# A fused attention and mixture kernel: the experts' second product in blocks of pairs of groups, for two of three token blocks

## The chip, the cores and the metric

The program runs on one core of a Trainium2 chip. The time is the device time of one execution, in microseconds (us); lower is better. The engines are TensorE (PE in the rows; its weight loads are PEld), VectorE (DVE), ScalarE (ACT), GpSimd (POOL) and SyncE (SP), which here issues all transfers.

## The reference, cut to what matters

```
# attention over 4 x 8 heads, 576 positions, block causal; then
x = attn.transpose(0, 2, 1, 3).reshape(2304, 512)
h = x @ w_in; x = (h * cos(h)) @ w_out             # first mixture layer
P = exp(x @ w_gate - max), 8 rounds of row and column normalisation
for e in range(8):                                 # second layer: all experts, all tokens
    h = maximum(x @ w1[e], 0)                      # 2304 x 512 @ 512 x 1024
    ye = h @ w2[e]                                 # 2304 x 1024 @ 1024 x 512
    out += P[:, e:e+1] * ye
```

## The kernel before, in words

Attention and the first layer take the first 600 us or so. The rest is the experts' loop, which the change touches. All products are in float32 precision by split operands: a tensor is held as a high part (rounded, `AF.Copy` to fp32r on ScalarE) and a low part (the difference, a subtraction on VectorE or GpSimd), and each product is three matmuls, high x high, high x low, low x high (`mm3`, L522 to L524).

The tokens are cut into three blocks of 768 (`HB`; `TB` is half of one), the 1024 hidden units of an expert into four slices `j` of 2 x 128 (`NJ`), so that there are 3 x 8 x 4 = 96 groups `(tb, e, j)`. Groups 0 to 31 are the first token block, 32 to 63 the second, 64 to 95 the third; all three use the same weights. A group does:

- The first product, x @ w1, as seven block products by the scheme of Strassen and Winograd: `A11 B11`, `S1 T1`, `S2 T2`, `A12 B21`, `S3 T3`, `A22 T4`, `S4 B22`, called P1 to P7 here in that order. The A and S are blocks and sums of blocks of w1, the B and T of the tokens. Each is 6 matmuls of 384 columns into the PSUM tiles `hx`, `hy`, `hz`. `hx` is accumulated over P1, P3, P5 and P6 and `hy` over P2 and P7; ScalarE copies `hx` out (`c`) behind P1, P3 and P5, so P3, P5 and P6 each wait for a copy, and VectorE adds `hy` to the third copy, for which P7 waits.
- ReLU and split of the four hidden quarters (`hidden_block`: `hh` on ScalarE, `hl` on VectorE).
- The second product of the group before, `y(g - 1, t)` for six token tiles t: 12 matmuls of 512 columns into `acc`, then VectorE adds P times `acc` to `oa` (L1006). `ys(0)` and `ys(1)` stand behind P5, `ys(2)` to `ys(5)` behind P7.
- The weights of the next group (`Weights(g + 1)`): the sums S1 to S4 on GpSimd, the splits `wbh`, `wbl`, `wah`, `wal` of w1 and `wv` of w2. `wload(g + 2)` loads two 512 KB tiles `stg` for the group after that. Every token block does this anew. All these tiles come out of one pool of 16 buffers (`wp`, tag `w`).

Ahead of a new token block `tprep` forms T1 to T4 of its tokens in ten sums on GpSimd and four splits, spread over the nine groups before it. The order of instructions on each engine is the order of the code (`manual_schedule`); each engine works through its own list and waits for what an instruction needs. At the end the last `y` calls run alone, and `oa` goes out.

## Time and profile before

| | |
|---|---|
| time, median of 3 runs | 2123.76 us (2123.02 to 2125.22) |
| the profiled execution: time, and its span | 2122.82 us, 2121.0 us |
| busy share of the span: TensorE, VectorE, ScalarE, GpSimd | 100%, 69%, 46%, 41% |
| mean transfer rate over the span | 72 GB/s |
| granted TensorE clock | 1.00 |

The span is the time from the first instruction to the last. Shares are averages over stages: attention, the first layer and the 96 groups have different loads.

### The profile page before, as it was taken

What the parts mean: (1) busy time and instruction counts of PE and PEld (TensorE: products, weight loads), DVE (VectorE), ACT (ScalarE), POOL (GpSimd) and SP (SyncE); (2) the same over time, 40 slices, a digit from 0 to 9 for tenths busy, and PEclk for the clock granted to TensorE, in tenths of its full rate; (3) what the DMA queues carried; (4) which work ended last, traced back from release to release, by engine and by line L of the source; (5) the groups of instructions that cost most, each with busy time, mean ns of one, the idle gap of its engine ahead of it and who ended that gap; (6) DMA issues with size and microseconds to landing.
All of it is one profiled execution on the core that took longest, in us unless ns stands there. A gap on an engine that the chain in (4) does not pass through costs nothing.

```text
span 2121.0 us, 29776 instructions
## 1 busy us (share of the span) xinstructions
PE 2112.4 (100%) x10959; PEld 1888.5 (89%) x10959; DVE 1456.0 (69%) x2411; ACT 981.8 (46%) x1852; POOL 875.8 (41%) x793
## 2 busy tenths in 40 slices
PE   9999999999999999999999999999999999999999
PEld 7888999999988888888988988889889888888898
DVE  7887876566768666666766666666776666666665
ACT  7887774344453444344343433433434344433342
POOL 4543233333334443435644434334554343343441
PEclk9999999999999999999999999999999999999999
DMA  6774320000011121211213212212113121121120
GB/s 168 186 190 127 101 89 1 6 11 30 11 50 60 66 74 60 78 62 60 80 46 108 76 60 74 66 60 80 60 62 107 60 74 67 60 80 60 62 78 30
DMA packets 77185, 152.84 MB, mean 72 GB/s; under 512 B 33232, under 2 KB 36816, under 8 KB 77040
## 3 DMA queue, kind: packets, MB, share of 16 engines
q1 hardware_dynamic: 77040, 150.95, 22.8%
q8 instruction: 86, 1.41, 0.3%
q14 instruction: 59, 0.48, 0.1%
HBM read 136.91 MB, written 4.87 MB: 67 GB/s over the span
## 4 chain that ended last, share of the span: by engine, by line
PE 92%; issue 4%; POOL 2%; DVE 1%; ACT 0%; DMA 0%; POOLq 0%; DVEq 0%
PE acc L522 13%; PE acc L524 13%; PE acc L523 13%; PE acc L774 7%; PE hx L524 6%; PE hx L522 6%; PE hx L523 6%; PE o L358 4%; PE hy L522 3%; PE hy L524 3%; PE hy L523 3%; PE h L522 2%; PE h L524 2%; PE h L523 2%; POOL jl L728 2%
## 5 line engine op out<-in xcount | busy, mean ns | idle before, releaser
L633 POOL TENSOR_TENSOR wv<-stg,wv 128x512 fp32r<-128x512 f32 x190 | 327.6, 1745 | 798.6 <-ACT wv L632 789.4
L522 PE MATMUL acc<-wv,hh 128*128 128x512 f32 x1152 | 456.7, 396 | 0.2 <-DVE oa L1000 0.2
L524 PE MATMUL acc<-wv,hl 128*128 128x512 f32 x1152 | 455.6, 395 | 0.0
L523 PE MATMUL acc<-wv,hh 128*128 128x512 f32 x1152 | 454.4, 394 | 0.0
L1006 DVE SCALAR_TENSOR_TENSOR oa<-acc,P,oa 128x512 f32<-128x512 f32 x540 | 378.6, 739 | 5.9 <-PE acc L524 4.3
L977 ACT ACTIVATE hh<-c 128x384 fp32r<-128x384 f32 x288 | 151.2, 525 | 411.2 <-DVE c L1065 167.6
L978 DVE SCALAR_TENSOR_TENSOR hl<-c,hh 128x384 fp32r<-128x384 f32 x288 | 164.9, 573 | 175.9 <-ACT hh L977 175.9
L524 PEld LDWEIGHTS acc<-wv,hl 128*128 128x128 f32 x1152 | 216.0, 187 | 53.8
L523 PEld LDWEIGHTS acc<-wv,hh 128*128 128x128 f32 x1152 | 215.9, 187 | 43.8
L522 PEld LDWEIGHTS acc<-wv,hh 128*128 128x128 f32 x1152 | 216.1, 188 | 43.1 <-DVE oa L1000 0.3
L1058 DVE TENSOR_TENSOR c<-hz,c 128x384 f32<-128x384 f32 x96 | 53.4, 556 | 195.8 <-PE hz L524 195.8
L1045 ACT ACTIVATE c<-hx 128x384 f32<-128x384 f32 x95 | 46.9, 494 | 267.5 <-PE hx L524 267.5
L728 POOL TENSOR_TENSOR jl<-raw,jh 128x512 fp32r<-128x512 f32 x63 | 92.3, 1466 | 189.5 <-ACT jh L723 169.5
L624 DVE TENSOR_TENSOR wal<-s,wah 128x1024 fp32r<-128x1024 f32 x89 | 159.7, 1794 | 0.0
L522 PE MATMUL hx<-th,wah 128*128 128x384 f32 x384 | 128.6, 335 | 0.0
L524 PE MATMUL hx<-th,wal 128*128 128x384 f32 x384 | 128.5, 335 | 0.0
L524 PE MATMUL hy<-xh,wal 128*128 128x384 f32 x384 | 128.5, 335 | 0.0
L522 PE MATMUL hy<-xh,wah 128*128 128x384 f32 x384 | 128.4, 334 | 0.0
L523 PE MATMUL hx<-tl,wah 128*128 128x384 f32 x384 | 128.3, 334 | 0.0
L523 PE MATMUL hy<-xl,wah 128*128 128x384 f32 x384 | 128.3, 334 | 0.0
L978 DVE SCALAR_TENSOR_TENSOR hl<-hx,hh 128x384 fp32r<-128x384 f32 x96 | 53.4, 557 | 104.4 <-ACT hh L977 101.7
L522 PE MATMUL h<-xh,jh 128*128 128x384 f32 x368 | 123.6, 336 | 0.0
(248 smaller groups left out, 4877.6 us busy)
## 6 DMA issues: line engine op xcount, KB each, us to landing
stg<-in_w_b_dram SPq DMA_DIRECT2D x192, 512.0 KB
st<-in_qk_dram SPq DMA_DIRECT2D x64, 144.0 KB
cw<-in_w_a_dram SPq DMA_DIRECT2D x17, 512.0 KB
v<-in_v_dram SPq DMA_DIRECT2D x31, 160.0 KB
tt<-inv SPq DMA_DIRECT2D x32, 144.0 KB
out_dram<-oa SPq DMA_DIRECT2D x18, 256.0 KB
kb<-qb SPq DMA_DIRECT2D x31, 144.0 KB
qb<-qa SPq DMA_DIRECT2D x31, 144.0 KB
```

The source lines that it names most:

```text
L358: nc.tensor.matmul(o[:, q0:q1], vt[:, c], e, start=c == 0, stop=True, skip_group_check=c > 0)
L522: nc.tensor.matmul(ps, lh, rh, start=first, stop=False, skip_group_check=go_on)
L523: nc.tensor.matmul(ps, lh, rl, start=False, stop=False, skip_group_check=go_on)
L524: nc.tensor.matmul(ps, ll, rh, start=False, stop=last, skip_group_check=go_on)
L624: eng.tensor_tensor(out=self.al, in0=self.s, in1=self.ah.bitcast(F32), op=ALU.subtract)
L633: eng.tensor_tensor(out=t[:, DM:2 * DM], in0=src, in1=t[:, 0:DM].bitcast(F32), op=ALU.subtract)
L728: eng.tensor_tensor(out=lo, in0=raw[units[n][1]][:, part * DM:(part + 1) * DM], in1=hi.bitcast(F32), op=ALU.subtract)
L774: nc.tensor.matmul(acc[half, b][:, at:at + w_], w[:, s], h[:, t0:t0 + w_], start=f == 0 and i == 0 and at == 0, stop=f == F1 - 1 and i == ...
L977: nc.scalar.activation(hh, src, AF.Relu)
L978: nc.vector.scalar_tensor_tensor(out=hl, in0=src, scalar=0.0, in1=hh.bitcast(F32), op0=ALU.max, op1=ALU.subtract)
L1006: nc.vector.scalar_tensor_tensor(out=o, in0=acc, scalar=p, in1=o, op0=ALU.mult, op1=ALU.add)
L1058: nc.vector.tensor_tensor(out=c[0], in0=z, in1=c[0], op=ALU.add)
```

## The change: what it does

The first token block stays as it was, but what it makes of the weights is kept. `store` writes the four split tiles of w1 of each group to DRAM (`W1D`, 1.84 MB a group), and `differences` replaces, on VectorE and in place, the w2 half of `stg` by four differences of its blocks and writes them to DRAM (`TD`, 0.52 MB a group). `hidden_block(g, 3)` and `hidden_block(g, 1)` move behind `ys(2)` and `ys(3)`; the pairs `hh`, `hl` now lie in shared tiles `hs`.

The second and third blocks load the split w1 from `W1D`, so the sums and splits of w1 fall away. The second product is done for pairs of groups p = (2p, 2p + 1): with the two groups the contraction is 2 x 256 deep, and the product is seven block products `X1`, `Y1`, `X2`, `Z`, `X3`, `Y2`, `X4` of 256 x 256 blocks, each for three token tiles. The 21 pieces (`TURN`), called items here, have 6 matmuls of 256 columns each; 11 of them stand between P1 to P7 of the next even group, 10 between those of the next odd group (`pair_group`). Their operands are, on the left, the hidden blocks A11, A12, A22 and their sums S1 to S4 (`both` on VectorE, then `high` on ScalarE and `low` on VectorE, 128 x 768 each), and on the right seven blocks of w2 (`w2_split`: high on ScalarE, low on GpSimd), loaded from DRAM into three or four places. Results are added to `oa` by 21 VectorE instructions of 256 columns (`collect`). Behind the last group follow two rounds of `pair_group` with items alone; at group 32 the old `y` calls stand between the products, and at group 33 nothing does.

```diff
+        W1D = [drw.tile([128, 14 * HK], F32, name=f"w1d{g}") for g in range(NA)]
+        TD = [drw.tile([128, 4, 2, HK], F32, name=f"td{p}") for p in range(NA // 2)]
...
+            def store(self):
+                for (at, n), t in zip(PARTS, (self.bh, self.bl, self.ah, self.al)):
+                    nc.sync.dma_start(out=W1D[self.g][:, at:at + n], in_=t[:, 0:n].bitcast(F32))
+            def differences(self, part, eng=nc.vector):
+                a, b = (t[:, DM:2 * DM] for t in stg[self.g])
+                b11, b12, b21, b22 = a[:, 0:HK], a[:, HK:2 * HK], b[:, 0:HK], b[:, HK:2 * HK]
+                for out, in0, in1 in (((b11, b12, b11), (b12, b12, b22)), ((b22, b22, b11), (b21, b21, b22)))[part]:
+                    eng.tensor_tensor(out=out, in0=in0, in1=in1, op=ALU.subtract)
+                if part:
+                    p, k = divmod(self.g, 2)
+                    for i, t in enumerate((a, b)):
+                        nc.sync.dma_start(out=TD[p][:, 2 * i:2 * i + 2, k, :],
+                                          in_=t.rearrange("p (o n) -> p o n", n=HK))
...
+        def w2_split(p, o):
+            if (p, o) in W2:
+                t, raw = W2[p, o], raws.pop((p, o))
+                nc.scalar.activation(t[:, 0:DM], raw, AF.Copy)
+                nc.gpsimd.tensor_tensor(out=t[:, DM:2 * DM], in0=raw, in1=t[:, 0:DM].bitcast(F32), op=ALU.subtract)
+                w2_load(raw)
...
+        TURN = [("X1", 0), ("X1", 1), ("X1", 2), ("Y1", 0), ("Y1", 1), ("Y1", 2), ("X2", 0), ("X2", 1), ("X2", 2),
+                ("Z", 0), ("Z", 1), ("X3", 0), ("X3", 1), ("X3", 2), ("Y2", 0), ("Y2", 1), ("Z", 2),
+                ("X4", 0), ("X4", 1), ("X4", 2), ("Y2", 2)]
...
+            def multiply(self):
+                name, t = self.todo.pop(0)
+                a, b, row, col = ITEMS[name]
+                ps, w, s = self.place(name, t), W2[self.p, b], slice(t * 128, (t + 1) * 128)
+                for k in range(2):
+                    new = k == 0 and name in ("X1", "Y1", "Z") and t != 1
+                    rh, rl = (w[:, i * DM + k * HK:i * DM + (k + 1) * HK] for i in range(2))
+                    mm3(ps, self.h[a][:, k, s], self.l[a][:, k, s], rh, rl, new, k == 1, go_on=True)
+                if t:
+                    self.collect(name, t, row, col)
+                if t == 1:
+                    self.collect(name, 0, row, col)
...
+        def pair_group(g, old, new, splits, ys):
...
+            if now:
+                product(g, x, "S2", "T2", False)
+                nc.scalar.activation(c[1], x, AF.Copy)
+                splits("T2")
+            if old:
+                if k == 0:
+                    old.high("S2")
+                else:
+                    old.high("A22")
+            if now and k:
+                w2_split(p, "B11")
+            items(1)
+            if old:
+                if k == 0:
+                    old.both("S4", "A12", "S2", ALU.subtract)
+                else:
+                    old.low("A22")
+            if now:
+                z = psz.tile([128, TB], F32, tag="z", name="hz")
+                product(g, z, "A12", "B21", True)
+                nc.vector.tensor_tensor(out=new.get("A11", k), in0=z, in1=c[0], op=ALU.add)
+                if k:
+                    new.relu("A11")
+                    new.high("A11")
+            if old and k == 0:
+                w2_split(p - 1, "T3")
+            if old and k == 0:
+                old.low("S2")
+            items(2)
+            if now:
+                product(g, x, "S3", "T3", False)
+                nc.scalar.activation(c[2], x, AF.Copy)
+                nc.vector.tensor_tensor(out=new.get("A22", k), in0=yy, in1=c[2], op=ALU.add)
...
                 product(g, x, "S3", "T3", False)
                 gate("S3")
+                Weights(g).differences(0)
                 nc.scalar.activation(c[2], x, AF.Copy)
                 nc.vector.tensor_tensor(out=c[2], in0=yy, in1=c[2], op=ALU.add)
-                hidden_block(g, 3, c[2])
                 splits("T3")
             ys(0)
             gate("y0")
+            Weights(g).differences(1)
...
             ys(2)
+            if now:
+                hidden_block(g, 3, c[2])
             if w and g:
                 w.lo_a(nc.gpsimd if g < 6 or left == 1 else nc.vector)
             ys(3)
+            if now:
+                hidden_block(g, 1, c[1])
...
             if w and g:
                 w.v(1)
+                w.store()
```

In the rows that follow, `p_...` is an item's PSUM tile, `w_...` a loaded or split weight tile, `raw` a hidden block, and `xh`, `xl` as the output or the weights of an item are the first token block's columns of these tensors, which are free by then and hold the items' left operands.

On TensorE, in a group of the second or third block before, the second product stands behind P5 in runs of 512 columns:

```order
L522 MATMUL hx<-th,wah 128x384
L523 MATMUL hx<-tl,wah 128x384
L524 MATMUL hx<-th,wal 128x384
L522 MATMUL acc<-wv,hh 128x512
L523 MATMUL acc<-wv,hh 128x512
L524 MATMUL acc<-wv,hl 128x512
```

At such a place after the change, an item stands between two products:

```order
L522 MATMUL hx<-th,w_16310 128x384
L523 MATMUL hx<-tl,w_16310 128x384
L524 MATMUL hx<-th,w_16479 128x384
L522 MATMUL p_16696<-w_16484,xh 128x256
L523 MATMUL p_16696<-w_16484,xh 128x256
L524 MATMUL p_16696<-w_16484,xl 128x256
L522 MATMUL hy<-xh,w_16480 128x384
L523 MATMUL hy<-xl,w_16480 128x384
L524 MATMUL hy<-xh,w_16481 128x384
```

The 72 matmuls of 512 columns of two groups have become 126 of 256, in runs of 6 or 12 between runs of 6 of 384; each still has a weight load of its own.

On VectorE, in a group of the first block, from the read of `hz` (P4) on; before:

```order
L1058 TENSOR_TENSOR c<-hz,c 128x384
L978 SCALAR_TENSOR_TENSOR hl<-c,hh 128x384
L613 TENSOR_TENSOR wbl<-stg,wbh 128x512
L615 TENSOR_TENSOR wbl<-stg,wbh 128x256
L1065 TENSOR_TENSOR c<-hy,c 128x384
L978 SCALAR_TENSOR_TENSOR hl<-c,hh 128x384
L1006 SCALAR_TENSOR_TENSOR oa<-acc,P,oa 128x512 x2
```

and with the change, with SyncE's list of such a group below it (before, SyncE had only the two loads of `stg` a group there):

```order
L1351 TENSOR_TENSOR c<-hz,c 128x384
L1001 SCALAR_TENSOR_TENSOR hs<-c,hs 128x384
L617 TENSOR_TENSOR wbl<-stg,wbh 128x512
L619 TENSOR_TENSOR wbl<-stg,wbh 128x256
L650 TENSOR_TENSOR stg<-stg 128x256 x2
L1359 TENSOR_TENSOR c<-hy,c 128x384
L1029 SCALAR_TENSOR_TENSOR oa<-acc,P,oa 128x512
```

```order
L654 DMA td_2418<-stg 128x2x256 x2
L590 DMA stg<-in_w_b_dram 128x1024 x2
L643 DMA w1d_2394<-wbh 128x768
L643 DMA w1d_2394<-wbl 128x768
L643 DMA w1d_2394<-wah 128x1024
L643 DMA w1d_2394<-wal 128x1024
```

Two differences stand ahead of the read of `hy` that P7 waits for, two more behind the first `oa`, and the loads of `stg` stand behind the stores of the differences in SyncE's list.

On VectorE with the change, in an even group of the second or third block (nothing like it stands there before), from `low` of S1 to the items X2:

```order
L1113 TENSOR_TENSOR xh<-raw,xl 128x768
L1162 SCALAR_TENSOR_TENSOR oa<-p_19027,P,oa 128x256 x2
L1162 SCALAR_TENSOR_TENSOR oa<-p_19053,P,oa 128x256
L1125 TENSOR_TENSOR raw<-raw 128x768 x2
L1223 TENSOR_TENSOR raw<-hz,c 128x384
L1113 TENSOR_TENSOR xl<-raw,xl 128x768
L1162 SCALAR_TENSOR_TENSOR oa<-p_19071,P,oa 128x256 x2
L1162 SCALAR_TENSOR_TENSOR oa<-p_19101,P,oa 128x256
```

S2 and S4 (L1125) stand behind the three collects of X1, and `low` of S2 (the second L1113), which X2 needs, behind the read of `hz`.

## Rows read from the trace of the kernel before

**Rows 1.** The page: span, busy time, granted clock and transfers in 40 slices.

```profile
span 2121.0 us, 29776 instructions
PE 2112.4 (100%) x10959; PEld 1888.5 (89%) x10959; DVE 1456.0 (69%) x2411; ACT 981.8 (46%) x1852; POOL 875.8 (41%) x793
...
PEclk9999999999999999999999999999999999999999
...
GB/s 168 186 190 127 101 89 1 6 11 30 11 50 60 66 74 60 78 62 60 80 46 108 76 60 74 66 60 80 60 62 107 60 74 67 60 80 60 62 78 30
```

**Rows 2.** The page: shares of the chain of work that ended last.

```profile
PE 92%; issue 4%; POOL 2%; DVE 1%; ACT 0%; DMA 0%; POOLq 0%; DVEq 0%
```

**Rows 3.** One line's instructions (one a group), 1105 to 2105 us: ns least/median/most, first, last.

```profile
L1058 DVE TENSOR_TENSOR c<-hz,c x64: 540/557/558, 1107.0 to 2097.5; 128x384 f32<-128x384 f32 x64
```

**Rows 4.** Busy time by engine in stretches (an early, a later, a second-block group; a load).

```profile
core 0: us, PE busy (x) PEld busy (x) DVE busy (x) ACT busy (x) POOL busy (x), PEclk, DMA share, GB/s
622.00:637.70 15.70, 15.70 (x82) 14.11 (x81) 11.53 (x26) 9.88 (x20) 8.92 (x8) 1.00 0.19 68
772.50:788.20 15.70, 15.70 (x80) 14.04 (x79) 10.33 (x17) 6.25 (x12) 6.33 (x7) 1.00 0.20 68
1119.29:1135.01 15.72, 15.72 (x80) 14.06 (x79) 10.34 (x17) 6.25 (x12) 6.35 (x7) 1.00 0.40 128
772.50:776.50 4.00, 4.00 (x25) 4.00 (x24) 2.07 (x4) 1.81 (x4) 3.92 (x5) 1.00 0.77 262
```

**Rows 5.** VectorE in order of time, the last `y` calls: start, us, instruction, [idle before].

```profile
2111.74 0.75 DVE L1006 SCALAR_TENSOR_TENSOR oa<-acc,P,oa 128x512 f32<-128x512 f32 x1 [0.65 <-PE acc L524]
...
2117.34 0.75 DVE L1006 SCALAR_TENSOR_TENSOR oa<-acc,P,oa 128x512 f32<-128x512 f32 x1 [0.65 <-PE acc L524]
```

**Rows 6.** The chain in order of time, first layer: 12 matmuls of 512, 12 of 256.

```profile
541.28 4.19 PE acc L774 x24
545.47 0.17 PE h L522
```

**Rows 7.** TensorE in order of time, attention: four matmuls of 256 columns, other weights each.

```profile
151.57 0.28 PE L330 MATMUL sq<-qb,kb 128*128 128x256 f32 x1
...
152.06 0.37 PE L330 MATMUL sr<-qb,kb 128*128 128x448 f32 x1
```

**Rows 8.** Their weight loads in order of time.

```profile
151.69 0.19 PEld L330 LDWEIGHTS sq<-qb,kb 128*128 128x128 f32 x1
151.82 0.19 PEld L331 LDWEIGHTS sq<-qa,ka 101*128 101x128 f32 x1
```

**Rows 9.** Groups of instructions: line, operation xcount | busy us, mean ns | idle before.

```profile
L1006 DVE SCALAR_TENSOR_TENSOR oa<-acc,P,oa 128x512 f32<-128x512 f32 x540 | 378.6, 739 | 5.9 <-PE acc L524 4.3 <-ACT oa L1005 1.5
L1065 DVE TENSOR_TENSOR c<-hy,c 128x384 f32<-128x384 f32 x96 | 52.7, 549 | 0.0
L1045 ACT ACTIVATE c<-hx 128x384 f32<-128x384 f32 x95 | 46.9, 494 | 267.5 <-PE hx L524 267.5
L632 ACT ACTIVATE wv<-stg 128x512 fp32r<-128x512 f32 x192 | 109.5, 616 | 0.0
L645 POOL TENSOR_TENSOR tt<-tt,xl 128x768 f32<-128x768 f32 x6 | 11.1, 1846 | 0.2
```

**Rows 10.** Single lines: ns least/median/most, first and last start (splits of three shapes).

```profile
L70 DVE TENSOR_TENSOR tl<-tt,th x9: 944/957/1556, 519.8 to 1602.4; 128x768 fp32r<-128x768 f32 x9
L624 DVE TENSOR_TENSOR wal<-s,wah x89: 1220/1807/1814, 561.9 to 2091.4; 128x1024 fp32r<-128x1024 f32 x89
L633 POOL TENSOR_TENSOR wv<-stg,wv x190: 1292/1300/2282, 615.3 to 2092.1; 128x512 fp32r<-128x512 f32 x190
L67 ACT ACTIVATE th<-tt x9: 828/831/841, 518.9 to 1601.0; 128x768 fp32r<-128x768 f32 x9
```

**Rows 11.** VectorE in order of time, group from about 772.4 us: behind P4, and its last part.

```profile
779.06 0.42 DVE L615 TENSOR_TENSOR wbl<-stg,wbh 128x256 fp32r<-128x256 f32 x1
779.40 0.55 DVE L1065 TENSOR_TENSOR c<-hy,c 128x384 f32<-128x384 f32 x1
...
786.51 1.81 DVE L624 TENSOR_TENSOR wal<-s,wah 128x1024 fp32r<-128x1024 f32 x1
```

**Rows 12.** ScalarE in order of time, start of the same group.

```profile
774.61 0.41 ACT L609 ACTIVATE wbh<-stg 128x256 fp32r<-128x256 f32 x1
775.73 0.49 ACT L1050 ACTIVATE c<-hx 128x384 f32<-128x384 f32 x1 [0.70 <-PE hx L524]
```

**Rows 13.** All engines in order of time: P4's last matmul, the next, P4's reader.

```profile
1200.84 0.33 PE L524 MATMUL hz<-xh,wbl 128*128 128x384 f32 x1
...
1201.01 0.33 PE L522 MATMUL hx<-th,wah 128*128 128x384 f32 x1
...
1201.28 0.56 DVE L1058 TENSOR_TENSOR c<-hz,c 128x384 f32<-128x384 f32 x1 [2.26 <-PE hz L524]
```

More of the change, by code (lines that the diff above doesn't have):

```diff
@@ L581, in wload @@
         def wload(g):
-            if g < NG:
+            if g < NA:
                 _, e, j = groups[g]
@@ L916, in moe1 @@
                         leftover[n]()
-        moe1()
+            return w0, w1
+        w0, w1 = moe1()
         fin = ctx.enter_context(tc.tile_pool(name="fin", bufs=1))
@@ L1008, in y, with w1_tiles @@
                 nc.sync.dma_start(out=out[row * 128:(row + 1) * 128, :], in_=o)
-        tgen, at = None, ""
-        for g in range(NG + 1):
-            now, w = g < NG, Weights(g + 1) if g + 1 < NG else None
+        W2 = {}
+        B_OPS = {"B11": (0, 0), "B21": (NJ, 0), "B22": (NJ, HK)}
+        T_OPS = {"T1": 0, "T3": 1, "T4": 2, "T2": 3}
+        def w1_tiles(g, some):
+            if g < NG:
+                for i in some:
+                    W2[g, i] = wp.tile([128, 2 * DM], F32R, tag="w", name="w1")
@@ new lines, in w1_load @@
+        def w1_load(g, some):
+            if g < NG:
+                for i in some:
+                    at, n = PARTS[i]
+                    nc.sync.dma_start(out=W2[g, i][:, 0:n].bitcast(F32), in_=W1D[g % NA][:, at:at + n])
+                if max(some) == 3:
+                    bh, bl, ah, al = (W2.pop((g, i)) for i in range(4))
+                    wa[g] = {n: (ah, al, i * HK) for i, n in enumerate(("S1", "S2", "S3", "S4"))}
+                    wa[g] |= {n: (bh, bl, i * HK) for i, n in enumerate(("A11", "A12", "A22"))}
@@ new lines, in w2_tiles, with w2_load @@
+        def w2_tiles(p, ops):
+            if 2 * p < NG:
+                for o in ops:
+                    W2[p, o] = wp.tile([128, 2 * DM], F32R, tag="w", name="w2")
+        W2_ORDER = ("B11", "T1", "T2", "B21", "T3", "B22", "T4")
+        raws, queue = {}, [(p, o) for p in range(NA // 2, NG // 2) for o in W2_ORDER]
+        def w2_load(place):
+            if queue:
+                p, o = queue.pop(0)
+                _, e, j = groups[2 * p]
+                raws[p, o] = place
+                dst = place.rearrange("p (k n) -> p k n", n=HK)
+                if o in B_OPS:
+                    f, c = B_OPS[o]
+                    src = w_b[e, j + f:j + f + 2, :, DM + c:DM + c + HK].rearrange("f p n -> p f n")
+                else:
+                    src = TD[p % (NA // 2)][:, T_OPS[o]]
+                nc.sync.dma_start(out=dst, in_=src)
@@ new lines, in w2_split @@
+        def w2_split(p, o):
[4 more added lines that the diff above has]
+                w2_load(raw)
+        halves = [t[:, c, 0:HB].rearrange("p (k n) -> p k n", n=TB) for t in (xh, xl) for c in range(NC)]
+        ITEMS = {"X1": ("A11", "B11", 0, 0), "Y1": ("S1", "T1", 1, 1), "X2": ("S2", "T2", 0, 1),
+                 "Z": ("A12", "B21", 0, 0), "X3": ("S3", "T3", 1, 1), "Y2": ("S4", "B22", 0, 1),
+                 "X4": ("A22", "T4", 1, 0)}
@@ new lines, in attention_moe_kernel, with last_ys @@
+        tgen, at = None, ""
+        pairs = {}
+        used = {(2 * (NA - 1) + i) % 3 for i in range(2)}
+        places = [f"hs{i}" for i in range(6) if i % 3 not in used]
+        rest = list(range(2 * TT))
+        def last_ys():
+            if rest:
+                y(NA - 1, rest.pop(0))
+                if not rest:
+                    places.extend(f"hs{i}" for i in range(6) if i % 3 in used)
+        for g in range(NG + 2):
+            now, w = g < NA, Weights(g + 1) if g + 1 < NA else None
@@ L1027, in splits @@
                     at = next(tgen, "")
+            if g >= NA:
+                p = g // 2
+                if g == NA:
+                    more = fin.tile([128, 4 * HK], F32, tag="s", name="s")
+                    w2_load(more[:, 0:DM])
+                    w2_load(more[:, DM:2 * DM])
+                    w2_load(post.tile([128, S], F32, tag="lt", name="raw", bufs=1)[:, 0:DM])
+                if 2 * p < NG and p not in pairs:
+                    pairs[p] = Pair(p)
+                pair_group(g, pairs.get(p - 1), pairs.get(p), splits, last_ys)
+                sums(1 + g % 2)
+                continue
             def ys(t):
@@ L1080, in attention_moe_kernel @@
                 nc.vector.tensor_tensor(out=c[1], in0=yy, in1=c[1], op=ALU.add)
-                hidden_block(g, 1, c[1])
                 gate("c1")
                 wload(g + 2)
+                if g >= NA - 2:
+                    w1_tiles(g + 2, range(4))
+                    w1_load(g + 2, range(4))
             ys(2)
+            if now:
+                hidden_block(g, 3, c[2])
             if w and g:
@@ L1087, in attention_moe_kernel @@
             ys(3)
+            if now:
+                hidden_block(g, 1, c[1])
             if w and g:
```

145 lines of the change are left out of this document (140 added, 5 removed).

## The prediction

> **What bounds the kernel now.** I read the page first. TensorE is busy for the whole span, and its granted clock is 1.00 in every slice, the upper level of 2.4 GHz [rows 1]; a busy PE need not be PE at its peak, so I looked at what ends last: TensorE holds 92% of the chain, GpSimd 2%, VectorE 1%, transfers nothing [rows 2]. Then the groups: the instruction that comes once a group starts 64 times between 1107.0 and 2097.5 us, so a group takes 990.5 / 63 = 15.72 us [rows 3], and in a stretch of that length TensorE is busy throughout while VectorE has 10.3 us, ScalarE 6.3 and GpSimd 6.4 [rows 4]. So in the two changed blocks a microsecond taken from TensorE's list is a microsecond gained, as long as nobody else then ends last.
>
> **What TensorE loses and gets.** A token tile of the old second product is 12 matmuls of 512 columns. With nothing else to do at the end, its reader comes every (2117.34 - 2111.74) / 4 = 1.400 us [rows 5], so 0.1167 us per 256 columns, or 0.2333 a matmul. Six tiles are 8.40 us, which leaves 15.72 - 8.40 = 7.32 us for P1 to P7, 1.046 each.
>
> A pair of groups gets 126 matmuls of 256 columns for 72 of 512, that is 32,256 columns for 36,864. What one of them costs decides the change. From below: 24 alternating matmuls take 4.19 us [rows 6], less 12 x 0.2333 leaves 0.116 each. From above: in attention four of 256, each with other weights, take (152.06 - 151.57) / 4 = 0.1225 [rows 7]. A weight load lasts 0.19 us; were loads one behind another, 126 of them would take 23.9 us and the pair would be far slower than before, but they start 0.13 apart, overlapping [rows 8], so they don't set the pace. I take 0.1175: a product's two matmuls with the same weights are nearer to the first case. Then 126 x 0.1175 = 14.8 us, and a pair takes 2 x 7.32 + 14.8 = 29.44 us for 31.44. That is 2.0 us a pair, **64 us in 32 pairs** (0.116: 70 us; 0.1225: 44 us). The change has no other source of gain: the sums and splits of w1 that fall away lie on engines that wait.
>
> The Trainium skill's page "TensorE: Matmul & The Clock Gate", section "Back-to-back issue gap", lists 518 cycles for 512 columns and 262 for 256, 0.216 and 0.109 us at 2.4 GHz. The rows show 0.233 for the first, and they decide; by the page's pair of figures the gain would be 72 x 0.216 - 126 x 0.109 = 1.8 us a pair, 58 us, much the same.
>
> **Whether the other engines keep up with a pair of 29.4 us.** VectorE: 21 collects of 256 columns, 6 sums of 384, 4 sums and 7 low parts of 768. A collect of 512 takes 0.739, a sum of 384 from PSUM 0.549, a low part of 768 undisturbed 0.957 [rows 9, 10]; at about 1.04 ns an element (0.957 less 0.549 over 384 is 1.06) a collect of 256 takes 0.47. Together 9.9 + 3.3 + 10.5 = 23.7 us of 29.4. ScalarE: 8 copies or ReLUs of 0.494, 9 of 768 at 0.83, 7 splits at 0.616, together 15.7. GpSimd: 7 low parts of 1.30, together 9.1. Transfers: 2 x 1.84 + 7 x 0.26 = 5.5 MB, at the 262 GB/s that a load of `stg` reaches [rows 4] 21 us. None is the bound by its sum, so what is left is the order.
>
> I walked the lists of both groups with these durations and 0.27 us from TensorE's going on to a reader's start [rows 13]. Two places are tight. In the odd group, ScalarE has ReLU and high part of A11 (1.66 us) in front of the third copy, for which P6 waits: P4 ends at 6.99 us, VectorE's sum at about 8.3 (the low part of A22 stands before it), the copy at about 10.5 to 10.7, and P6 is due at 10.85. In the even group X2 is due at 9.44 and the low part of S2 comes at about 9.25. Margins of 0.2 us. Behind P6 stand all of TensorE's later items.
>
> What makes them uncertain is GpSimd. The low part of `wal` takes 1.22 us at least and 1.807 in the median, when GpSimd works at `wv`; GpSimd's own goes from 1.300 to 2.282 [rows 10]. So VectorE instructions with both inputs in SBUF and GpSimd's wait for each other. All 11 of the pair's 768-wide VectorE instructions are of that kind. From below such meetings cost nothing; from above one whole GpSimd split, 1.30 us, a pair. The splits stand in GpSimd's list just behind the tight VectorE instructions, so mostly VectorE comes first. I take 0.25 us a pair, **8 us**.
>
> The Trainium skill's page "SBUF — State Buffer", section "Who interferes with whom", says that a VectorE instruction with two SBUF inputs and a GpSimd one that reads SBUF exclude each other for their whole length. The trace agrees (1.22 to 1.807 us). By that rule the price depends only on who comes first, which is my second rival.
>
> **Transition and tail.** At group 33 no old work stands between the products. P6 follows P5 at once, but must wait for the sum of A11, ReLU, high part and copy: 0.27 + 0.55 + 0.83 + 0.83 + 0.49 = 2.97 us and some signals from the end of P4, less P5's 1.05: 2 us. Group 32 has its six old tiles before P5, so P6 waits 0.27 + 0.49 there, 0.8. Together **3 us**. At the end 21 items (14.8 us) run without products between them, and S1's sum, high and low (0.96 + 0.83 + 0.96, behind VectorE's other sum) have only three items of X1, 2.1 us, to hide under; the same for S2. I count 2 us for each, **4 us**; below zero is excluded, since the old tail had no wait but the last reader's.
>
> **The first block.** It does the old work and more. VectorE gets four differences of 256 columns, 0.42 each [rows 11], 1.7 us on 10.3 of 15.7 [rows 4]. Two stand before the sum that P7 waits for: that sum, at 779.40, 7.0 us into the group, moves to about 8.0, less what the moved `hidden_block` spares; it ends at 8.6 and P7 is due at 9.07. So hidden, except where GpSimd or VectorE is late already: the first six groups, with 11.5 us on VectorE and low parts on GpSimd [rows 4], and the nine with `tprep`'s sums of 1.85 us on GpSimd [rows 9]. From 0 to 1.7 us in 5 groups and 0.6 in 9, 0 to 14; I take **4 us**. The same ten sums stand in GpSimd's list in the second block, ahead of the pairs' splits: 0 to 18 us if each shows, I take **4 us**.
>
> Transfers: 1.05 MB in and 2.36 MB out a group, 3.4 MB. The wait that is new: SyncE's loads of `stg` for g + 2 stand behind the stores of the differences, which wait for VectorE, about 10 us into the group. Behind them the four stores wait too, but nobody waits for those soon. At 262 GB/s differences and loads (1.57 MB) take 6 us and land by about 17, that is 1.3 us into the next group, where ScalarE needs the second half at 774.61 - 772.4 = 2.2 [rows 12]; late by more than about 0.9, it holds the copy at 3.3 and P5. So hidden with 1 us to spare.
>
> **The sum.** 2122.8 (the profiled execution: 1.8 us around its span, 0.9 under the median of the runs) - 64 + 3 + 4 + 8 + 4 + 4 = 2081.8; on the median's footing **2083 us**, 1.9% faster. A kernel like this can be told from no change at about 0.2%, 4 us.
>
> **The rivals.**
> - *Slower: the first block is bound by transfers.* The most that the trace moved for longer is 190 GB/s in a slice of 53 us [rows 1]; with a third of it short packets, but stores to DRAM of this size it doesn't show at all. At 190, 3.4 MB take 17.9 us, so the next loads land late, group after group: 32 x 2.2 = 70 us, for 2149. It decides from 3.4 MB in 15.72 + 41 / 32 = 17.0 us, 200 GB/s. Against it: 262 over the 4 us of a load with the engines busy 77%. 8%.
> - *VectorE's chain becomes the bound of the pairs.* If GpSimd comes first once a pair, 32 x 1.3 = 42 us for 8: 2117; twice a pair would be 2158. For it: margins of 0.2. Against it: the order above. 17%, a third of it within 0.2% or slower.
> - *Nothing shows but transition and tail, at 0.116:* 2123.8 - 70 + 7 = 2061. 12%.
> - Something else that ends slower (a wait that I didn't see in the transition's 11 buffer changes): 3%.
>
> My forecast has 60%, between 2066 and 2100. Faster by over 0.2%: 0.60 + 0.11 + 0.12 = 0.83; within: 0.05; slower: 0.12. The range reaches from the third rival to the second: 2062 to 2116.
>
> **What the changed profile would show.** Matmuls of 256 columns start 0.116 to 0.12 apart; a pair takes 29.4 to 30 us, against 31.44. TensorE's idle time lies at P6 of odd groups and at X2, a few tenths each; at group 33 and at the end, 2 to 4 us. Groups 6 to 22 still take 15.72. Wrong would be: groups of the first block over 16 us (transfers or the differences), pairs over 30.5 with TensorE waiting for VectorE's low parts (the lock), or 256-column matmuls 0.13 apart.

## The result and the profile after

The changed kernel takes **2098.43 us** (median of 4 runs, 2097.37 to 2099.77) where the kernel before takes 2123.39 beside it: a ratio of 0.988, 95% interval 0.9867 to 0.9892. The direction and the range hold; the forecast of 2083 is 15.4 us too low. The profiled execution took 2099.2 us with a span of 2097.3.

The page of the changed kernel, its parts on busy time, slices, chain and groups (those that answer to [rows 1, 2, 9]):

```profile
span 2097.3 us, 34781 instructions
PE 2067.8 (99%) x12687; PEld 1944.3 (93%) x12687; DVE 1573.7 (75%) x2733; ACT 1046.8 (50%) x1852; POOL 832.5 (40%) x631
...
GB/s 167 185 186 133 108 91 1 6 11 31 1 106 196 205 226 217 210 228 215 206 218 235 170 197 182 197 180 184 165 178 182 206 203 173 187 201 179 191 174 111
...
PE 92%; DVE 5%; DMA 1%; issue 1%; ACT 1%; POOL 0%; SPq 0%; DVEq 0%; ACTq 0%
...
L1162 DVE SCALAR_TENSOR_TENSOR oa<-p,P,oa 128x256 f32<-128x256 f32 x648 | 280.7, 477 | 66.2 <-PE p L524 64.4
```

TensorE still holds 92% of the chain, but VectorE now has 5% where it had 1% [rows 2], and transfers 1% where they had nothing. Transfers reach 235 GB/s in a slice and lie above the 190 of [rows 1] for ten slices in a row. The collect of 256 columns costs 0.477 us, as forecast (0.47).

The sum of A11, one a group in the two changed blocks (it answers to [rows 3]: ns least/median/most, first and last start), the busy time in the stretch of one undisturbed pair [rows 4], and, in that pair, the first of twelve matmuls of 256 columns and the matmul that follows the twelve, in order of time [rows 6, 7]:

```profile
L1223 DVE TENSOR_TENSOR raw<-hz,c x64: 548/551/559, 1125.3 to 2065.7; 128x384 f32<-128x384 f32 x64
```

```profile
1254.80:1284.40 29.60, 29.60 (x212) 29.60 (x211) 22.43 (x40) 14.55 (x25) 11.00 (x8) 1.00 0.55 188
```

```profile
1263.45 0.28 PE L522 MATMUL p<-w,xh 128*128 128x256 f32 x1
...
1264.88 0.34 PE L522 MATMUL hx<-th,w 128*128 128x384 f32 x1
```

A group takes (2065.7 - 1125.3) / 63 = 14.93 us in the mean, for 15.72. Undisturbed pairs take less: from the first matmul of P2 to that of the next group it is 15.153 us in an even group and 14.433 in an odd one, so a pair is 29.587 us (sums of the unrounded times), with TensorE busy throughout. A matmul of 256 columns is (1264.88 - 1263.45) / 12 = 0.119 us; from the pair it is (29.587 - 2 x 7.32) / 126 = 0.1186.

Where the rest went shows in a ledger of the two traces, by the first matmul of P2 in each group (us):

| stretch | before | after | difference |
|---|---|---|---|
| start to group 0 | 596.66 | 597.48 | +0.8 |
| groups 0 to 5 | 98.19 | 109.35 | +11.2 |
| groups 6 to 31 | 408.72 | 410.81 | +2.1 |
| groups 32 and 33 | 31.44 | 25.84 | -5.6 |
| groups 34 to 55 | 345.84 | 326.03 | -19.8 |
| groups 56 to 64 | 141.48 | 146.45 | +5.0 |
| groups 65 to 94 | 471.75 | 443.80 | -28.0 |
| group 95 to the end | 26.94 | 37.52 | +10.6 |

Two stretches stand out. Groups 0 to 5 lose 11 us, and groups 56 to 64, which at the pace of an undisturbed pair would take 5 x 15.153 + 4 x 14.433 = 133.5 us, take 13.0 more. GpSimd makes the sums of `tprep` for the third block from the end of group 55 on, and the splits follow in group 63, so these are the groups that hold them.

What TensorE waits for, the four largest rows (engine, what, us in total, times, longest):

```profile
PE p L524 <- DVE xl L1113: 7.7, 6, 2.1
PE hx L522 <- ACT c L1343: 5.2, 3, 2.1
PE hy L522 <- DVE c L1359: 2.1, 3, 0.8
PE hx L522 <- ACT c L1234: 2.0, 2, 1.8
```

The first row is low parts that come late, mostly in groups 56 to 62, the second P5 in the first groups, the third P7 in groups 0, 24 and 28, the fourth mostly P6 in group 33. They add up to 17 us; a part of the loss is no wait but the lower clock behind one, as shown below. The four executions of the changed kernel have mean granted clocks of 0.998, 0.997, 0.995 and 0.995, in the order of their times from 2097.37 to 2099.77 us, where the kernel before has 1.00. The waits that I had expected in every pair, at P6 of odd groups and at X2, are not among them.

### The profile page after: what moved, and what is told of

It reads as the page before. It is cut to its first block, busy times and chain, and to the rows that moved or that the text cites. A ratio compares the mean times of both kernels' runs of the same rounds, so it can differ in the third digit from the quotient of the medians.

```text
span 2097.3 us, 34781 instructions
## 1 busy us (share of the span) xinstructions
PE 2067.8 (99%) x12687; PEld 1944.3 (93%) x12687; DVE 1573.7 (75%) x2733; ACT 1046.8 (50%) x1852; POOL 832.5 (40%) x631
## 4 chain that ended last, share of the span: by engine, by line
PE 92%; DVE 5%; DMA 1%; issue 1%; ACT 1%; POOL 0%; SPq 0%; DVEq 0%; ACTq 0%
PE acc L794 10%; PE p L524 7%; PE p L523 7%; PE p L522 7%; PE hx L522 6%; PE hx L523 6%; PE hx L524 6%; PE o L358 4%; PE acc L522 4%; PE acc L524 4%; PE acc L523 4%; PE h L522 3%; PE h L524 3%; PE h L523 3%; PE hy L522 3%; PE hy L523 3%
## 5 line engine op out<-in xcount | busy, mean ns | idle before, releaser
L1078 POOL TENSOR_TENSOR w<-s,w 128x512 fp32r<-128x512 f32 x150 | 237.3, 1582 | 418.7 <-ACT w L1077 399.4
L1162 DVE SCALAR_TENSOR_TENSOR oa<-p,P,oa 128x256 f32<-128x256 f32 x648 | 280.7, 477 | 66.2 <-PE p L524 64.4
L524 PE MATMUL p<-w,xl 128*128 128x256 f32 x894 | 253.9, 284 | 7.7 <-DVE xl L1113 7.7
L523 PE MATMUL p<-w,xh 128*128 128x256 f32 x834 | 235.0, 282 | 0.0
L522 PE MATMUL p<-w,xh 128*128 128x256 f32 x834 | 234.6, 281 | 0.0
L637 POOL TENSOR_TENSOR wv<-stg,wv 128x512 fp32r<-128x512 f32 x62 | 111.8, 1823 | 223.3 <-ACT wv L636 223.3
L524 PEld LDWEIGHTS p<-w,xl 128*128 128x128 f32 x894 | 170.6, 191 | 9.1 <-DVE xl L1113 8.9
L523 PEld LDWEIGHTS p<-w,xh 128*128 128x128 f32 x834 | 158.1, 190 | 0.0
L522 PEld LDWEIGHTS p<-w,xh 128*128 128x128 f32 x834 | 157.7, 189 | 0.0
L522 PE MATMUL acc<-wv,hs 128*128 128x512 f32 x384 | 154.0, 401 | 0.9 <-DVE oa L1023 0.9
L524 PE MATMUL acc<-wv,hs 128*128 128x512 f32 x384 | 152.8, 398 | 0.0
L523 PE MATMUL acc<-wv,hs 128*128 128x512 f32 x384 | 152.5, 397 | 0.0
L522 PE MATMUL p<-w,xl 128*128 128x256 f32 x510 | 145.1, 284 | 1.0 <-ACT xl L1109 1.0
L523 PE MATMUL p<-w,xl 128*128 128x256 f32 x510 | 145.0, 284 | 0.0
L1029 DVE SCALAR_TENSOR_TENSOR oa<-acc,P,oa 128x512 f32<-128x512 f32 x168 | 122.7, 742 | 13.1 <-PE acc L524 12.8
L522 PE MATMUL hx<-th,w 128*128 128x384 f32 x384 | 129.5, 337 | 2.0 <-ACT c L1234 2.0
L524 PE MATMUL hx<-th,w 128*128 128x384 f32 x384 | 128.7, 335 | 0.0
L524 PE MATMUL p<-w,xh 128*128 128x256 f32 x450 | 127.8, 284 | 0.2 <-DVE xh L1113 0.2
```

Of the source, the lines that this page charges most:

```text
L522: nc.tensor.matmul(ps, lh, rh, start=first, stop=False, skip_group_check=go_on)
L523: nc.tensor.matmul(ps, lh, rl, start=False, stop=False, skip_group_check=go_on)
L524: nc.tensor.matmul(ps, ll, rh, start=False, stop=last, skip_group_check=go_on)
L637: eng.tensor_tensor(out=t[:, DM:2 * DM], in0=src, in1=t[:, 0:DM].bitcast(F32), op=ALU.subtract)
L1029: nc.vector.scalar_tensor_tensor(out=o, in0=acc, scalar=p, in1=o, op0=ALU.mult, op1=ALU.add)
L1078: nc.gpsimd.tensor_tensor(out=t[:, DM:2 * DM], in0=raw, in1=t[:, 0:DM].bitcast(F32), op=ALU.subtract)
```

## The experiments

All times are medians beside runs of the kernel before on the same chip. "The changed kernel" is 2098.43.

**1. The first block's part alone.** The differences and stores are made, the second product stays as it was: the loop over pairs is left out, and all blocks split w1 as before.

```
-        for g in range(NG + 2):
-            now, w = g < NA, Weights(g + 1) if g + 1 < NA else None
+        for g in range(NG + 1):
+            now, w = g < NG, Weights(g + 1) if g + 1 < NG else None
...
-                pair_group(g, pairs.get(p - 1), pairs.get(p), splits, last_ys)
-                sums(1 + g % 2)
-                continue
```

> The changed first block (differences, stores to DRAM, later hidden blocks) with the old groups in the second and third block; what is stored is not read. Theory: what the first block lost (0.8 us to its start, 11.2 in groups 0 to 5, 2.1 in groups 6 to 31, by the two traces) is due to its own additions: 14 us over the kernel before, 2137 us (2134 to 2141). Rival: part of it comes from what the pairs bring (loads of kept weights, their buffers), then under 2130.

It took 2137.55 us (2136.28 to 2138.74), ratio 1.0064 (1.0049 to 1.0079): 14.1 us slower than the kernel before. The ledger's first three rows add up to the same 14.1. So the additions to the first block cost 14 us by themselves, and the changed second and third block bring 39.

**2. Loads ahead of stores.** In the first block SyncE's loads of the next `stg` stand ahead of the differences' stores, and the differences stand behind the sum that P7 reads.

```
-                Weights(g).differences(0)
                 nc.scalar.activation(c[2], x, AF.Copy)
...
             gate("y0")
-            Weights(g).differences(1)
+            wload(g + 2)
+            if g < NA:
+                Weights(g).differences(0)
             if w and g:
                 w.hi_a()
             ys(1)
+            if g < NA:
+                Weights(g).differences(1)
...
                 gate("c1")
-                wload(g + 2)
```

> The changed kernel with the loads of stg for g + 2 ahead of the differences and their stores, and all four differences behind the sum that P7 waits for. Theory: groups 0 to 2 wait because those loads stand behind stores that wait for VectorE (two waits of 2.4 us and the lower clock behind each), and groups 24 and 28 because two differences stand ahead of that sum (0.9 and 1.0): 6 to 11 us less, 2087 to 2092. Rival: VectorE's own work in the first groups (normalisation and differences) is what ends last wherever the loads stand: 2 us less, 2096.

2088.79 us (2088.04 to 2090.48), ratio 0.9836 (0.9821 to 0.9851): 9.6 us less than the changed kernel. What it undoes stands in the chain of the changed kernel, in order of time (start, us, what), groups 0 and 1:

```profile
609.39 0.34 DVE stg L650
...
611.02 0.44 DVE stg L650
...
611.47 0.38 SPq L654
...
612.45 5.74 DMA stg<-in_w_b_dram
...
618.22 0.42 ACT wbh L613
618.63 0.39 ACT c L1343
...
619.06 0.44 PE hx L522
```

VectorE makes the last difference at 611.0, SyncE then issues the stores (L654), behind them the loads (L590), the second lands at 618.2, ScalarE takes its high part (L613) and behind that makes the copy for which P5 waits (L1343). SyncE's own rows say how far the queue held the loads back, here of the changed kernel, and then of the one with the loads first:

```profile
610.21 1.64 SPq L654 DMA_DIRECT2D td<-stg  x2
611.94 0.92 SPq L590 DMA_DIRECT2D stg<-in_w_b_dram  x2
```

```profile
597.96 0.33 SPq L590 DMA_DIRECT2D stg<-in_w_b_dram  x1
610.03 1.30 SPq L654 DMA_DIRECT2D td<-stg  x2
```

In the kernel before, where SyncE's list had only loads, the two of this group had gone out long ahead of it:

```profile
580.22 2.25 SPq L586 DMA_DIRECT2D stg<-in_w_b_dram  x2
```

With the loads first the second of them goes out at 597.96 (the first at 589.60), so both buffers were free by then; only the place in the list made the loads wait until 612. Groups 1 and 2 take 16.6 and 16.4 us with the edit for 20.6 and 20.1, and 16.6 and 16.2 before the change, though the same bytes are moved. Groups 0 to 5 take 101.9 us for 109.4, and groups 6 to 31 409.2 for 410.8: most of what P7's late sum cost in groups 24 and 28 (16.6 and 16.7 us, now 15.8 and 15.9) has gone too. The edit moves the loads and the differences together, so the 9.6 us are not divided between the two by a run; groups 1 and 2, which waited at P5, are the loads' part, and 24 and 28, which waited at P7, the differences'.

**3 and 4. The sums of the third block.** In the one, GpSimd's sums stand inside the pairs instead of behind each group's program; in the other they stay where they are but each is two memsets of the same tile, so T1 to T4 of the third block are left out.

```
             elif old:
                 w2_split(p - 1, "T4")
+                sums(1)
             items(2)
...
                 old.low("S2")
+                sums(2)
             items(2)
...
-                sums(1 + g % 2)
```

```
             def op(out, in0, in1, what):
+                if tb == 2:
+                    for _ in range(2):
+                        eng.memset(out, 0.0)
+                    return
                 eng.tensor_tensor(out=out, in0=in0, in1=in1, op=what)
```

> The changed kernel with the ten sums of tprep on GpSimd, in the second block, moved from the end of a group to behind the split of T3 (two, even groups) and of T4 (one, odd groups), where VectorE reads PSUM. Theory: groups 56 to 64 take 13.0 us more than other pairs because these sums and VectorE's S1 and S3 exclude each other: 9 to 12 us less, 2086 to 2090. Rival: GpSimd has no room for 10 x 1.85 us beside the pairs' splits, and the weights' low parts come late wherever the sums stand: no change, 2096 to 2099.

> The changed kernel with each of the ten sums of tprep for the third block replaced by two memsets on GpSimd at the same place (the third block's T1 to T4 are left out). Theory: it is the reading of SBUF by both engines that delays VectorE's S1 and S3, and a memset reads nothing: S1 and S3 go back to 0.96 us and 9 to 12 us are gained, 2086 to 2090. Rival: GpSimd's list is late, which is the same with memsets of like length: over 2094.

The first took 2086.7 us (2086.42 to 2086.99), ratio 0.9825 (0.981 to 0.984), 11.7 less than the changed kernel; the second 2087.78 (2086.95 to 2088.79), ratio 0.9832 (0.9815 to 0.9848), 10.6 less. Groups 56 to 64 take 135.0 and 135.9 us for 146.5, so 11.4 and 10.6 us lie there. What is left over the 133.5 of undisturbed pairs, 1.5 us with the sums moved, lies in group 63, where the splits of T2 to T4 stand, and a little in 64. The changed kernel in group 58, VectorE, GpSimd and TensorE in order of time:

```profile
1500.16 4.33 DVE L1122 SCALAR_TENSOR_TENSOR raw<-raw 128x768 f32<-128x768 f32 x2
1504.41 2.03 DVE L70 TENSOR_TENSOR xl<-tt,xh 128x768 fp32r<-128x768 f32 x1
1506.37 0.94 DVE L1113 TENSOR_TENSOR xl<-raw,xh 128x768 fp32r<-128x768 f32 x1
...
1499.85 1.29 POOL L1078 TENSOR_TENSOR w<-raw,w 128x512 fp32r<-128x512 f32 x1 [1.77 <-ACT w L1077]
1501.10 2.56 POOL L665 TENSOR_TENSOR tt<-xh,tt 128x768 f32<-128x768 f32 x1
1503.62 2.00 POOL L1078 TENSOR_TENSOR w<-s,w 128x512 fp32r<-128x512 f32 x1
...
1507.36 0.38 PE L524 MATMUL p<-w,xl 128*128 128x256 f32 x1 [2.14 <-DVE xl L1113]
```

S1 and S3 (L1122) take 4.33 us together, 1.8 and 2.6. The 1.8 of S1 is no loss against other pairs: in an undisturbed pair, too, S1 runs beside one of GpSimd's splits and takes 1.8, and S3 0.95. New are the 2.6 of S3, beside GpSimd's sum, which takes 2.56 for 1.85 [rows 9], and the split of `tprep` behind it, 2.03 for 0.957 [rows 10], beside another of GpSimd's splits. The low part of S1 starts 3.5 us later in its group than in an undisturbed pair, and TensorE waits 2.14. The same line from 1462 to 1592 us in the changed kernel, with the sums moved, and with memsets (there it is L1126), and the memsets themselves:

```profile
L1122 DVE SCALAR_TENSOR_TENSOR raw<-raw x8: 1796/2202/2609, 1468.4 to 1568.6; 128x768 f32<-128x768 f32 x8
```

```profile
L1122 DVE SCALAR_TENSOR_TENSOR raw<-raw x10: 942/946/1798, 1468.4 to 1590.4; 128x768 f32<-128x768 f32 x10
```

```profile
L1126 DVE SCALAR_TENSOR_TENSOR raw<-raw x10: 937/946/1798, 1467.8 to 1590.8; 128x768 f32<-128x768 f32 x10
...
L667 POOL MEMSET tt<- x18: 737/742/750, 1468.8 to 1559.2; 128x768 f32 x18
```

Two memsets hold GpSimd for 1.48 us, four fifths of a sum (1.85), at the same place of its list, and S3 is back at about 0.95; the 1.8 that stays as the longest is S1's beside the split. So it is not GpSimd's time or the place in its list alone that delays VectorE, but a GpSimd operation that reads SBUF while VectorE reads two tiles there. The Trainium skill says just this on its page "SBUF — State Buffer", section "Who interferes with whom" (such pairs exclude each other, a GpSimd operation that only writes does not); the runs agree, 2.61 us against 0.95 for S3.

**5 and 6. The tail.** VectorE was busy for 19.7 of the 21.4 us between the last first product (P7 of group 95) and TensorE's last matmul. One kernel gives the last pair's low parts of A12, S3 and A22 to GpSimd; the other keeps TensorE busy where it waits.

```
             def low(self, o, keep=False):
                 self.l[o] = halves.pop(0)
-                nc.vector.tensor_tensor(out=self.l[o], in0=self.get(o), in1=self.h[o].bitcast(F32), op=ALU.subtract)
+                eng = nc.gpsimd if self.p == NG // 2 - 1 and o in ("A12", "S3", "A22") else nc.vector
+                eng.tensor_tensor(out=self.l[o], in0=self.get(o), in1=self.h[o].bitcast(F32), op=ALU.subtract)
```

```
             def items(n):
+                if old and g == NG and old.todo[0] in (("Y1", 0), ("X2", 0)):
+                    ps = psz.tile([128, 128], F32, tag="z", name="busy")
+                    for _ in range(11 if old.todo[0][0] == "Y1" else 9):
+                        nc.tensor.matmul(ps, ones, ones, start=True, stop=True)
```

> As the changed kernel, but in the last pair of groups alone GpSimd and no longer VectorE takes the low parts of A12, S3 and A22 (three operations of 768 columns). My theory: the 24.9 us from the last pair's first product to the end are bound by VectorE, which is busy for 19.7 of the 21.5 us from 2072.5 to 2094; three operations of about 0.95 us less, of which one meets a GpSimd operation again: 2 to 3 us faster than the changed kernel, about 2096 (2095 to 2097). Rival: the tail is bound by the order of items and collects, or by the lower granted clock, whoever computes the low parts: no change, 2098.4 within 0.5.

> As the changed kernel, with 11 and 9 matmuls of 128 columns that nobody reads, put ahead of the two places of the last pair at which TensorE waits for VectorE (1.29 and 0.77 us), so that it is busy there and its granted clock does not fall to 0.51 to 0.55 behind them. My theory (VectorE ends last in the tail) expects the matmuls behind to run at 0.117 us for 256 columns where they took 0.2133, and the end to move by 0.5 us at most: 2098 to 2098.7. Rival: the lower clock is what makes the tail long; then some 3 us come back, about 2095.5.

The first took 2099.89 us (2099.15 to 2101.48), ratio 0.9889 (0.9872 to 0.9905): no gain, rather 1.5 lost. The second took 2098.16 (2097.87 to 2099.86), ratio 0.9881 (0.9866 to 0.9895): no difference. By the times alone my theory fell in the first and stood in the second; the traces say why. The chain of the kernel with the low parts on GpSimd, near its end:

```profile
2083.83 1.85 POOL xl L1114
2085.68 1.23 POOLq L1430
2086.91 1.98 POOL w L1078
2088.89 1.80 POOL xh L1114
```

VectorE's load fell to 16.8 us, but the low parts now stand in GpSimd's list with two splits of weights between them (the first runs during the piece called POOLq), and the chain runs there. The tail, from the start of the last matmul of P7 to that of TensorE's last, is 21.6 us, for 21.4 in the changed kernel. The four traces with the low parts on VectorE and their edit far from the end (2, 3, 4 and 7) have 20.13 us there, all four alike, whether the clock is 1.00 throughout (3) or 0.92 in the mean (2). The chain of experiment 2 in the tail shows what sets it:

```profile
2063.25 1.81 DVE raw L1122
...
2065.08 0.85 ACT xl L1109
...
2065.96 0.96 DVE xl L1113
2066.92 1.18 DVE oa L1162 x3
2068.09 0.88 DVE raw L1125
...
2073.72 1.19 DVE xl L1113
```

From 2063.3 to 2074.9 it is VectorE, with one step of ScalarE; the first sum takes 1.81 because a GpSimd split stands in its way. From then on TensorE ends last without a wait. With 132 matmuls at 0.1186 (15.7 us) the tail's waits are 4.5 us in these four. The 1.2 us more of the changed kernel lie in the clock, in busy time by stretch (the column behind the engines is the granted clock), here in the changed kernel:

```profile
2071.60:2077.70 6.10, 4.60 (x35) 4.19 (x34) 5.56 (x8) 2.43 (x4) 2.67 (x2) 1.00 0.29 90
2077.70:2084.50 6.80, 6.60 (x30) 6.05 (x29) 6.22 (x11) 4.03 (x7) 3.91 (x4) 0.50 0.11 39
2084.50:2093.00 8.50, 8.50 (x73) 8.50 (x71) 7.89 (x15) 0.69 (x1) 0.62 (x1) 1.00 0.17 62
```

and with the added matmuls:

```profile
2073.30:2093.60 20.30, 20.30 (x174) 20.30 (x172) 18.82 (x32) 7.16 (x11) 7.94 (x5) 1.00 0.20 67
```

After gaps of 1.29 and 0.77 us between two starts the granted clock is 0.50, the level of 1.2 GHz, for 6.8 us, and 30 matmuls start there where 57 would fit. With the added matmuls it is 1.00 and the tail is 20.3 us. So the clock costs 1.0 to 1.2 us (21.37 less 20.33 or 20.13) and not the 3 of the rival, since VectorE's chain would hold TensorE up anyway; the added matmuls took 4.3 us where the gaps were 2.1, so they gain nothing beyond that. In the medians the gain of 1 us doesn't show beyond the spread of the runs.

**7. The third copy first.** In group 33 ScalarE makes ReLU and high part of A11 behind the third copy.

```
                 nc.vector.tensor_tensor(out=new.get("A11", k), in0=z, in1=c[0], op=ALU.add)
-                if k:
+                if k and old:
                     new.relu("A11")
                     new.high("A11")
...
                 nc.vector.tensor_tensor(out=new.get("A22", k), in0=yy, in1=c[2], op=ALU.add)
+                if k and not old:
+                    new.relu("A11")
+                    new.high("A11")
```

> As the changed kernel, but in group 33, the first of the pairs, ScalarE makes ReLU and high part of A11 behind the third copy of the block's input and not ahead of it. The third copy is what P6 waits 2.14 us for at 1137.4; the two operations ahead of it take about 1.3 us. Theory: the wait shrinks to about 0.8 us, 2097.1 in all (2096.6 to 2097.6). Rival: A11 itself is then late for the items of group 34, and the time goes there: 2098.4.

2096.99 us (2095.0 to 2098.09), ratio 0.9872 (0.9858 to 0.9887): 1.4 less, as expected, though the runs' ranges overlap. ScalarE in the changed kernel, in order of time:

```profile
1137.37 0.84 ACT L1118 ACTIVATE raw<-raw 128x768 f32<-128x768 f32 x1 [0.64 <-DVE raw L1223]
1138.24 0.84 ACT L1109 ACTIVATE xh<-raw 128x768 fp32r<-128x768 f32 x1
1138.99 0.47 ACT L1234 ACTIVATE c<-hx 128x384 f32<-128x384 f32 x1
```

The copy (L1234), for which P6 waits, starts at 1138.99 though P5 had long ended. With the edit this wait is 0.6 us and groups 32 and 33 take 25.08 us for 25.84, and the groups behind them 0.6 less.

**8 and 9. All of it, and without the GpSimd low parts.** The edits of 2, 3, 5 and 7 together, and then of 2, 3 and 7 alone.

> As the changed kernel with four edits at once: the loads of the next weights ahead of the differences' stores (9.6 us faster by itself), the sums of the third block inside the pairs and not behind them (11.7), the low parts of the last pair on GpSimd, and the third copy first. If these are four places that have nothing to do with each other, their gains add up: 2098.4 - 9.6 - 11.7 - 2.5 - 1.3 = 2073.3 (2071 to 2077). If the first two share a cause, such as a queue that stays late, the sum is less: about 2082.

> The all-in-one kernel with the last pair's low parts back on VectorE: loads ahead of stores, sums inside the pairs, third copy first. In the traces the stretch from the last first product to TensorE's last matmul was 20.1 us in the four kernels whose low parts stayed on VectorE and where TensorE's clock stayed up or came back early, and 21.6 where GpSimd took them, whose own queue held them back. Theory: the tail is a chain on VectorE, and on GpSimd it is only a worse one; 1.4 us come back, 2076.6 (2075 to 2078). Rival: the 1.2 us are the clock's alone and come and go with it; then no change from the all-in-one kernel, 2078.

2077.99 us (2076.85 to 2078.41), ratio 0.9783 (0.9768 to 0.9798), and 2076.93 (2075.54 to 2078.26), ratio 0.9782 (0.9769 to 0.9796). The gains of 2, 3 and 7 add up to 22.8 us, the second of these kernels gains 21.5: within 1.3 us the three causes are separate. The first lies 1 us above the range that I gave it, since its sum had 2.5 us for GpSimd's low parts, and they cost time. Its tail is 20.13 us and that of the first 21.57, so GpSimd's low parts cost 1.4 us there; the medians lie 1.1 apart, within their ranges.

**10. Differences on GpSimd in groups 3 to 5.** This is the kernel of experiment 9 with one more edit. After experiment 2 these groups still took 17.0, 17.9 and 18.2 us, for 16.2, 16.8 and 17.1 before the change.

```
-                Weights(g).differences(0)
+                Weights(g).differences(0, nc.gpsimd if 2 < g < 6 else nc.vector)
...
-                Weights(g).differences(1)
+                Weights(g).differences(1, nc.gpsimd if 2 < g < 6 else nc.vector)
```

> As the kernel with three edits, and in groups 3 to 5 of the first block GpSimd makes the four differences of the weights (128x384, about 0.55 us each on VectorE). VectorE is busy for 18.8 of 20 us there, and the three groups take 17.0, 17.9 and 18.2 us where the kernel before took 16.2, 16.8 and 17.1. Theory: VectorE's added 2.2 us a group are what is late; without them about 2 us come back, 2074.5 (2073.5 to 2076). Rival: GpSimd's operations slow VectorE's down where the two meet, by 0.8 us each time as in the third block; then nothing comes back, 2076.6, or it gets longer.

2074.87 us (2074.17 to 2075.76), ratio 0.9771 (0.9758 to 0.9785), 2.1 less than experiment 9 in the median and the lowest of all, though the ranges of the two overlap by 0.2 us. In the trace the three groups take 17.4, 16.7 and 17.7, 1.2 us less in all, of 1.4 by which the two profiled executions differ: VectorE's differences were part of what was late there, and group 3 gets longer. So the trace bears out the theory's sign and about half of its size; the other 0.7 of the medians are not shown to be the edit's.

## Why the prediction was right in direction and 15 us too low

The forecast's sum went from 2122.8 to 2081.8, 41 us; the profiled execution took 2099.2, 23.6 less. Step by step:

| step | forecast | measured |
|---|---|---|
| 126 matmuls of 256 for 72 of 512, and stalls in the pairs | -64 + 8 | -59.3 |
| groups 32 and 33, and group 34 | +3 | +2.8, +0.6 |
| tail | +4 | +5.7 (+4.5 without the clock) |
| first block | +4 | +14.1 |
| sums of `tprep` in the second block (groups 56 to 64) | +4 | +13.0 |

The measured column adds up to -23.1.

- **The items.** 0.1186 a matmul, between the bounds and near the 0.1175 that I took; 32 x (31.44 - 29.587) = 59.3. The 8 us of stalls weren't there: undisturbed pairs have no wait at all. Net the step is 3 us off, to the good side, so it hid 3 us of what the other steps missed.
- **Transition and tail** came as worked out: 25.84 - (2 x 7.32 + 8.40) = 2.8, and waits of 4.5 us, which the lower clock made 5.7.
- **The first block is the step that failed.** "SyncE's loads of `stg` for g + 2 stand behind the stores of the differences, which wait for VectorE, about 10 us into the group", and "so hidden with 1 us to spare": the mechanism is named and rightly, the place in time was read from a group at 772 us, and in groups 0 to 5 VectorE's list is later. From the start of P1, as the forecast counts, the loads of group 0 were issued 611.94 - 596.41 = 15.5 us into the group, not 10, and those of groups 1 to 5 between 14.4 and 18.7, so the spare microsecond was gone. The groups from 6 on, from which I had read it, behave as forecast (loads at 10.3 in most, and 15.72 us each, apart from 24 and 28 and 0.2 us or less in two more). Experiment 2 shows 9.6 of the 14 to be the order of loads and differences; experiment 10 adds 1 to 2 of the rest. The sign that I had named, groups of the first block over 16 us, could not tell by itself: groups 1 to 5 took 16.2 to 17.1 us before the change.
- **The sums of `tprep`** were given 4 us out of a range of 0 to 18. They took 13. The sums themselves took 11.4 of these, by experiment 3; the rest stays in groups 63 and 64. I had the lock between VectorE and GpSimd as a rival for all pairs, at 1.3 us a pair. In pairs where GpSimd has only its splits the two meet as well (S1 takes 1.8), but TensorE waits for nothing; where sums of 1.85 us join them, in the even groups 56, 58, 60 and 62, it is 11.4 / 4 = 2.9 us a pair, part of it the lower clock. The price of several meetings in a row, S1, S3 and what stands behind them, was not in the sum.
- **The rivals.** Transfers don't bound the first block: they reach 415 GB/s (below), groups 6 to 22 still take 15.72 us, and in the two waits where a load ends last, in groups 1 and 2, it is one issued late, as experiment 2 shows. VectorE's chain is the bound in four pairs of 32, a little in the one behind them, and in the tail, not in the rest. The third rival, nothing but transition and tail, had 2061 at 0.116 a matmul; at 0.1186 that is 32 x 126 x 0.0026 = 10.5 us more, 2071.5, and experiment 10 comes within 4 us of it.

## What to carry to other kernels

A list of transfers is a queue of its own: a load that stands behind a store waits for whoever computes what is stored, even when its buffer is free, so put loads first and read the margin from the worst group, not from a typical one. Where work moves from one engine to another, count the meetings of VectorE operations with two tiles in SBUF and GpSimd operations that read SBUF one by one at each place, since one or two added GpSimd sums cost 1.7 to 4.0 us an even group there, the lower clock included, while in the 30 groups behind them the meetings with GpSimd's splits cost TensorE nothing. At the end of a program, where one engine has the list, look first whether the other engine's list has room at that moment: here it had none, and moving the low parts cost 1.4 us.

## What I had not expected

A wait of about 2 us can cost more than its length. The changed kernel by stretches: a wait in group 1 of the first block and what follows, the same in group 58, and the stretch behind P6's wait in group 33 (the columns are those of [rows 4]):

```profile
617.00:620.20 3.20, 1.14 (x6) 1.14 (x7) 0.74 (x2) 2.61 (x6) 1.59 (x3) 1.00 1.02 415
620.20:624.00 3.80, 3.80 (x12) 2.72 (x11) 3.50 (x4) 1.71 (x4) 3.72 (x4) 0.55 1.03 418
...
1504.90:1507.30 2.40, 0.32 (x3) 0.12 (x1) 2.40 (x3) 0.49 (x1) 0.73 (x1) 1.00 1.03 385
1507.30:1510.30 3.00, 2.94 (x12) 2.94 (x13) 2.97 (x7) 0.91 (x2) 0.00 (x0) 0.57 0.89 356
1510.30:1514.00 3.70, 3.70 (x27) 3.70 (x27) 2.83 (x7) 0.94 (x2) 2.01 (x1) 0.89 0.02 5
...
1139.50:1142.50 3.00, 2.98 (x17) 2.98 (x18) 1.98 (x3) 2.11 (x4) 2.00 (x1) 1.00 0.22 75
```

TensorE is busy for 1.14 of 3.2 us, and in the next 3.8 us its granted clock is 0.55 and matmuls of 512 columns start 0.43 us apart instead of 0.23; in group 58 it is 0.57 behind a wait of 2.14 us. Group 58 takes 19.114 us, 3.96 over its undisturbed 15.153: two starts lie 2.42 us apart there for 0.12, so 2.3 of them are the wait, and (1 - 0.57) x 3.0 + (1 - 0.89) x 3.7 = 1.7 the clock. It is not so each time. In the changed kernel's trace, ahead of the tail, six waits put two starts 2.09 to 2.42 us apart; four of them were followed by the lower level, and two were not, P6's in group 33 (1.00 in the last row) and the one in group 56. The wait of group 58 stands with the same 2.42 us in the trace of experiment 2, and there the clock stays at 1.00. In the tail two shorter gaps, 1.29 and 0.77 us with two matmuls between, were followed by the lower level for 6.8 us; in experiment 3 the same gaps were not. What decides it these runs don't show. One such stretch costs up to 1.7 us, so a difference of 1 to 2 us between two of these kernels is better read from the ledger of their traces than from their medians. And transfers reached 415 GB/s beside busy engines, far over the 262 from which I had worked.
